# Chunks and halves of the second and third batch, and a new DVE order in the last batch, in an attention and two-level MoE kernel

## The chip, the cores and the metric

One core of a Trainium2 chip runs the program. The metric is the device time of one execution in microseconds (us): the median of three runs of the kernel before is 514.22, from 513.57 to 514.29.

## The reference, cut to what matters

Eight batches of 576 tokens go through attention with eight heads of 64, in which keys and values are means over 8 neighbours (72 of each). The 4608 rows of 512 numbers that come out go through a mixture of experts: a group is chosen, then one of its four experts, and the output is scaled by both probabilities.

```python
scores = scale * np.matmul(q, k_p.transpose(0, 1, 3, 2))
scores = scores - np.max(scores, axis=-1, keepdims=True)
attn = np.exp(scores); attn = attn / (np.sum(attn, axis=-1, keepdims=True) + 1e-09)
out_attn = np.matmul(attn, v_p)
...
h = np.maximum(xg[mask_e] @ w1[g, e], 0.0)
ye = h @ w2[g, e]
out[tok_idx] = combined[:, None] * ye
```

## The kernel before, in words

A batch goes through two stages that overlap with its neighbours: the attention of batch b+1 runs between the expert products of batch b. One main expert is taken for a whole batch (its number steers the loads of the weights); the few tokens that belong to another are gathered at the end, in a part that the code calls `Left`.

**Order.** Every engine executes its instructions in the order in which they were written. That order stands in strings of pieces: START and FIRST (batch 0), SECOND (batch 1), STEADY (batches 2 to 6), LAST (batch 7). `run` (L953) reads a string and calls one method per piece. The letter ahead of the dot says whose: `a` attention of the batch, `n` of the next, `x` of the one after that, `m` the batch's expert products, `w` those of the next, `p` of the one before, `l` the `Left` part. `n.sc:2` is thus the score products of chunk 2 of the next batch.

**Attention.** Tokens come in chunks: a batch below EARLY (3) has five, of 128 (the last 64); the others have three, of 192. For a chunk, DVE transposes q (`qb`, L322), TensorE makes the scores (`sc`, L336: per 32 tokens eight products of 72 columns), DVE takes the maxima (`mx`, L348) and subtracts them (`sd`, L357), ACT does exp (`ex`, L362), DVE sums and inverts (`su_`, L368 to L370), POOL normalises (`nm`, L375), DVE transposes the probabilities (`pt`, L382). The piece `sb` is `sd` and `ex` in one. Then TensorE multiplies with the values for half a batch at a time (`av`, L396): halves of 256 and 320 tokens in the batches below EARLY, of 288 and 288 in the others. ACT and DVE make a high and a low part of the result (L401, `avd` L412 or L414).

**Experts.** `load` brings a quarter of a weight matrix by SP, `cast` (ACT, L579) takes its high part and `lo` (L585, on POOL, or on DVE with `:v`) the remainder. `up:f:h` is 12 products for slice f of the hidden layer and half h of the tokens (L602), then relu on ACT (L604). `upd:f:h` is DVE's low part of the result (one instruction at L610 for half 0, three at L615 for half 1). Three PSUM banks are shared by the groups of 12 products, so the fourth group behind needs a bank that ACT and DVE have read out. `down` (L631, L642) is the second matrix.

**The last batch.** While TensorE does batch 7's experts, `Left` is planned, all of it on DVE but for small things: the generator `place` (L708 to L772) gives one step per `l.step` (copies of products at L734, running sums at L738 and L739, positions at L751 to L760). `which` (L774) computes on DVE which batch and which expert come next; SP reads these numbers into registers (L786 to L788), and then `fetch_x` (L834) issues two DMAs that are addressed by them. `xtiles` clears their targets by two POOL memsets (L824). When they have landed, `whole` (L848, POOL for odd chunks, DVE for even) adds the two parts and `turn` (L858) transposes them on TensorE. These transposes stand in TensorE's order between `up:7:1`, the products of `rows` (L816), and `down:12`.

Of the kernel before, what the change touches and what calls it, by code (L numbers as in the profile page):

```python
# [1000 lines left out]
```

## Time and profile before

| | |
|---|---|
| median of three runs | 514.22 us (513.57 to 514.29) |
| profiled execution | 514.15 us |
| its span | 512.4 us |
| mean granted clock of TensorE | 0.993 |
| busy: PE / PEld | 501.1 us (98%) / 440.1 us (86%) |
| busy: DVE / ACT / POOL | 345.6 (67%) / 206.3 (40%) / 281.6 us (55%) |

PE is TensorE's products, PEld its weight loads, which overlap the products; DVE, ACT and POOL are the other three engines, SP issues DMAs. The span runs from the first to the last instruction; the execution's time is 1.75 us longer. Since products are pipelined, their recorded durations overlap, and a group's cost is read from the distance between two starts. In the rows of the timeline a bracket gives the idle time ahead of the group and what ended it.

### The profile page before, as it was taken

To read this page: it belongs to the slowest core of one execution; us is meant where nothing else is said; L and a number is where in the kernel's file an instruction comes from. 1 tells how busy PE (TensorE), PEld (TensorE's weight loads), DVE (VectorE), ACT (ScalarE), POOL (GpSimd) and SP (SyncE) were. 2 spreads that over 40 slices of the span, in tenths; PEclk is the share of its full clock that TensorE was granted. 3 is DMA by queue.
4 is the path that set the end of the run, shared out by engine and by line. 5 is a ranking of instruction groups with operands and counts; after the bars stand their busy time and mean duration, and the time that the engine had idled before them with its cause. 6 is when DMAs were issued, how large, how long until landed. Compare 5 with 4: busy or idle time off the path is not lost.

```text
span 512.4 us, 14902 instructions
## 1 busy us (share of the span) xinstructions
PE 501.1 (98%) x6085; PEld 440.1 (86%) x6085; DVE 345.6 (67%) x928; ACT 206.3 (40%) x385; POOL 281.6 (55%) x246
## 2 busy tenths in 40 slices
PE   8899999999999999999999999999999999998996
PEld 6688987998889978899789988899789988898976
DVE  6876877899385869486784768476784764199702
ACT  2354432545216542455216551455325551344212
POOL 2386666576518595476828585476947471830400
PEclk9799999999999999999999999999999999999999
DMA  8699299685428966954197615985055100923751
GB/s 279 191 260 205 24 280 236 124 192 137 77 92 242 265 106 176 318 150 80 29 308 213 151 26 138 368 311 89 1 191 192 43 3 22 304 96 114 271 172 58
DMA packets 118110, 83.70 MB, mean 163 GB/s; under 512 B 71034, under 2 KB 93818, under 8 KB 117784
## 3 DMA queue, kind: packets, MB, share of 16 engines
q1 hardware_dynamic: 113408, 75.67, 54.7%
q10 hardware_dynamic: 4600, 7.02, 4.0%
q8 instruction: 49, 0.80, 0.7%
q14 instruction: 21, 0.17, 0.1%
q0 software_dynamic: 32, 0.04, 0.0%
HBM read 77.28 MB, written 28.53 MB: 206 GB/s over the span
## 4 chain that ended last, share of the span: by engine, by line
PE 76%; DVE 10%; DMA 5%; ACT 2%; POOL 2%; issue 2%; SPq 1%; ACTq 0%; DVEq 0%; POOLq 0%
PE mm L602 30%; PE mm L631 27%; PE mm L642 4%; PE sc L396 4%; PE sc L336 4%; DMA vv<-in_v_dram 2%; DMA sw<-in_moe_w_dram 2%; PE tp L429 1%; PE mm L663 1%; POOL w L585 1%; DVE s L368 1%; DVE ht L615 1%; DVE pT L382 1%; PE tp L425 1%; DVE p L357 1%
## 5 line engine op out<-in xcount | busy, mean ns | idle before, releaser
L631 PE MATMUL mm<-w,ht 128*128 128x512 f32 x744 | 172.6, 385 | 0.0
L585 POOL TENSOR_TENSOR w<-sw,w 128x1024 fp32r<-128x1024 f32 (+2 forms) x86 | 145.2, 1711 | 33.7 <-ACT w L579 29.2
L631 PEld LDWEIGHTS mm<-w,ht 128*128 128x128 f32 x744 | 136.8, 189 | 25.2 <-issue 6.4
L602 PE MATMUL mm<-xb,w 128*128 128x288 f32 (+1 forms) x768 | 109.6, 294 | 1.7 <-DVE ht L610 1.7
L602 PEld LDWEIGHTS mm<-xb,w 128*128 128x128 f32 x768 | 100.7, 189 | 6.1 <-ACT w L579 2.2
L602 PE MATMUL mm<-xa,w 128*128 128x288 f32 (+1 forms) x768 | 100.2, 283 | 0.5 <-ACT xa L401 0.5
L602 PEld LDWEIGHTS mm<-xa,w 128*128 128x128 f32 x768 | 95.5, 190 | 2.2 <-ACT xa L401 0.9
L604 ACT ACTIVATE ht<-mm 128x288 fp32r<-128x288 f32 (+2 forms) x128 | 51.9, 410 | 87.1 <-PE mm L602 85.4
L375 POOL TENSOR_TENSOR p<-p,su 128x864 f32<-128x864 f32 (+2 forms) x30 | 40.3, 1343 | 78.6 <-DVE su L370 67.7
L579 ACT CAST w<-sw 128x1024 fp32r<-128x1024 f32 x64 | 66.7, 1042 | 31.5 <-DMA sw<-in_moe_w_dram 29.0
L615 DVE SCALAR_TENSOR_TENSOR ht<-mm,ht 128x64 fp32r<-128x64 f32 (+4 forms) x192 | 37.7, 252 | 25.8 <-ACT ht L604 25.5
L636 ACT ACTIVATE y<-mm,gm 128x512 f32<-128x512 f32 x31 | 21.2, 684 | 66.4 <-PE mm L631 66.4
L362 ACT ACTIVATE p<-p 128x864 f32<-128x864 f32 (+2 forms) x30 | 23.4, 780 | 37.5 <-DVE p L357 29.6
L368 DVE TENSOR_REDUCE s<-p 128x12 f32<-128x864 f32 (+2 forms) x30 | 25.8, 861 | 15.1 <-ACT p L362 15.1
L382 DVE STREAM_TRANSPOSE pT<-p 128x960 f32<-128x960 f32 (+2 forms) x30 | 29.2, 972 | 8.0 <-POOL p L375 7.2
L610 DVE SCALAR_TENSOR_TENSOR ht<-mm,ht 128x288 fp32r<-128x288 f32 (+1 forms) x64 | 26.9, 422 | 10.4 <-ACT ht L604 10.4
L642 PE MATMUL mm<-w,ht 128*128 128x512 f32 x128 | 29.5, 381 | 0.0
L336 PEld LDWEIGHTS sc<-kT,qT 64*32 64x32 f32 x2176 | 23.7, 105 | 6.3 <-issue 3.5
L336 PE MATMUL sc<-kT,qT 64*32 64x72 f32 x2176 | 28.5, 229 | 0.5 <-DVE qT L322 0.2
L675 DVE TENSOR_TENSOR y<-mm,y 64x512 f32<-64x512 f32 x8 | 5.5, 682 | 33.6 <-ACT y L647 20.2
L396 PE MATMUL sc<-pT,v 32*64 32x288 f32 (+2 forms) x384 | 26.9, 409 | 0.2 <-DVE p L357 0.2
L396 PE MATMUL tp<-pT,v 32*64 32x288 f32 (+2 forms) x384 | 26.9, 409 | 0.0
(227 smaller groups left out, 568.8 us busy)
## 6 DMA issues: line engine op xcount, KB each, us to landing
sw<-in_moe_w_dram SPq DMA_DIRECT2D x72, 512.0 KB
vv<-in_v_dram SPq DMA_DIRECT2D x27, 320.0 KB
q<-in_q_dram SPq DMA_DIRECT2D x112, 72.0 KB
kv<-in_k_dram SPq DMA_DIRECT2D x14, 512.0 KB
out_dram<-y ACTq DMA_DIRECT2D x23, 256.0 KB
xscr<-xa SPq DMA_DIRECT2D x5, 1152.0 KB
xscr<-xb SPq DMA_DIRECT2D x5, 1152.0 KB
xscr<-xb SPq DMA_DIRECT2D x3, 1280.0 KB
```

Source lines behind the costliest of these rows:

```text
L336: nc.tensor.matmul(ps[x][32 * g:32 * g + 32, SP * t:SP * t + SP], lhsT=s.qT[c][64 * x:64 * x + 64, g, 32 * t:32 * t + 32], rhs=s.kT[64 * x ...
L368: red(out=two[:, :, :, 0], in_=p.rearrange("p t (x s) -> p t x s", x=2), axis=AX.X, op=ALU.add)
L375: (nc.vector if eng == "v" else nc.gpsimd).tensor_tensor(out=p, in0=p, in1=bc(s.su[c][:, 0:w], SP), op=ALU.mult)
L382: nc.vector.transpose(out=s.pT[:, :, o:o + n].rearrange("p j (t i) -> p t j i", i=32), in_=probs[:, z:z + n // 32].rearrange("p t (j i) -> ...
L396: nc.tensor.matmul(banks[a][64 * x:64 * x + 64, 0:n], lhsT=s.v6[32 * a:32 * a + 32, 5 if x and i == 0 else j, :], rhs=s.pT[32 * a:32 * a + ...
L579: nc.scalar.copy(out=s.w[m, j][0], in_=raw)
L585: (nc.vector if eng == "v" else nc.gpsimd).tensor_tensor(out=wl[:, i:i + n], in0=s.raw[m, j][:, i:i + n], in1=wh[:, i:i + n].bitcast(F32), ...
L602: nc.tensor.matmul(ps[:, 0:n], lhsT=l[:, kc, fs], rhs=apart(s.a.xt[hf][:, r, kc]), start=(kc == 0 and i == 0), stop=(kc == 3 and i == 2))
L604: nc.scalar.activation(out=halves(ht[:, sl]), in_=joined(ps[:, 0:n]), func=AF.Relu)
L615: stt(out=ht[:, at:at + hi - lo], in0=ps[:, a, lo:hi], scalar=0.0, in1=ht[:, t + lo:t + hi].bitcast(F32), op0=ALU.max, op1=ALU.subtract)
L631: nc.tensor.matmul(ps, lhsT=s.ht[f][:, 640 * l + o:640 * l + o + 128], rhs=apart(s.w[2, f // 2][r][:, f % 2, :]), start=(i == 0), stop=(i ...
L642: nc.tensor.matmul(ps, lhsT=s.ht[f][:, 512:640], rhs=apart(s.w[2, f // 2][r][:, f % 2, :]), start=(i == 0), stop=(i == 15))
```

## The change

EARLY becomes 1, so that batches 1 and 2 have three chunks of 192 and halves of 288. The old way of routing and of the low part stays for batches below 3, under the new name OLD. FIRST and SECOND lose the pieces of chunks 3 and 4, and others move. LAST is written anew, and so are the first two steps of `place`. One line less stands ahead of the functions, so a line of before has a number lower by one after the change.

```diff
-EARLY = 3
+EARLY, OLD = 1, 3
...
-m.lo:2:2:p:2 n.kt m.cast:2:3 m.up:5:1 m.upd:5:1 a.count a.gm_:p a.keep_x n.sc:0 n.mx:0 n.sb:0 n.qb:1 m.lo:2:3:p:2 m.up:6:1 ...
+m.lo:2:2:p:2 n.kt m.cast:2:3 m.up:5:1 m.upd:5:1 a.count a.gm_:p a.keep_x m.lo:2:3:p:2 m.up:6:1 w.load:1:0 w.load:1:1 m.upd:6:1 n.sc:0 n.mx:0 n.sb:0 n.qb:1 m.up:7:1 m.upd:7:1 n.su_:0 n.nm:0:p
...
+m.down:0 w.load:1:2 m.down:1 w.load:1:3 n.sc:1 n.pt:0 n.mx:1 n.sb:1 n.qb:2 m.down:2 m.store:0 n.su_:1 n.nm:1:p x.load_v x.load_k m.down:3 w.split:1:0:p:2 m.down:4 n.sc:2 n.mx:2 n.pt:1 n.sb:2 w.split:1:1:p:2
...
 LAST = """
-m.load:2:3 m.load:2:2 m.up:0:0 p.tail m.upd:0:0 m.lo:1:2:v m.up:0:1 l.step m.upd:0:1 m.up:1:0 l.step l.step m.upd:1:0 m.up:1:1 l.step l.step m.upd:1:1 l.xtiles
-m.up:2:0 m.cast:2:1 l.step m.upd:2:0 l.step m.up:2:1 l.step m.upd:2:1 l.step m.up:3:0 l.step l.step m.upd:3:0 m.up:3:1 l.step l.step m.upd:3:1
-m.up:5:0 l.step l.step l.step l.step m.upd:5:0 m.lo:1:3 m.cast:2:2 m.up:4:0 l.step l.step l.which m.lo:2:2:v m.upd:4:0 m.lo:2:1:v
-m.up:6:0 m.cast:2:0 m.upd:6:0 m.up:5:1 m.lo:2:0:v m.up:4:1 m.up:6:1 m.cast:2:3 l.fetch_x l.tiles m.upd:5:1 m.upd:4:1 m.upd:6:1 l.slots m.down:0 m.down:1 l.fetch_a:1
+l.step m.load:2:3 m.load:2:2 m.lo:1:2 m.lo:1:3 m.up:0:0 p.tail m.upd:0:0 m.up:0:1 l.step m.cast:2:0 m.upd:0:1 m.lo:2:0 m.up:1:0 l.step l.step m.upd:1:0 m.up:1:1 l.step l.step m.upd:1:1 l.xtiles
+m.up:2:0 m.cast:2:1 l.step m.upd:2:0 m.lo:2:1:v m.up:2:1 l.step m.upd:2:1 m.up:3:0 l.step l.step m.upd:3:0 m.up:3:1 l.step l.step m.cast:2:2 m.upd:3:1
+m.up:5:0 l.step l.step m.upd:5:0 m.up:4:0 l.step l.step l.step l.step m.upd:4:0 m.up:6:0 l.step m.upd:6:0 m.up:5:1 l.step l.which m.upd:5:1 m.up:4:1 m.lo:2:2:v m.upd:4:1 m.up:6:1 m.cast:2:3 l.fetch_x l.tiles m.upd:6:1 l.slots m.down:0 m.down:1 l.fetch_a:1
...
-                if s.b < EARLY:
+                if s.b < OLD:
...
             nc.gpsimd.affine_select(out=tri, in_=ones, ...)
+            nc.gpsimd.iota(s.colf, [[0, 4], [1, BS]], ...)
+            yield
             nc.scalar.copy(out=trir, in_=tri)
             nc.scalar.copy(out=onesr, in_=ones)
             yield
-
-            nc.gpsimd.iota(s.colf, [[0, 4], [1, BS]], ...)
```

POOL at the end of batch 6 and the start of batch 7, before; the rows are engine-order rows of line, operation, output, inputs and tile, and an `x3` is three alike in a row. `w` is the remainder of a weight quarter, `pT` and `xr` the targets of `fetch_x`:

```order
L585 TENSOR_TENSOR w<-sw,w 128x1024 x2
L715 AFFINE_SELECT kb<-ones 128x128
L720 IOTA kb 128x128
L824 MEMSET pT 128x2304
L824 MEMSET xr 128x2304
L585 TENSOR_TENSOR w<-sw,w 128x1024
L764 IOTA meta 128x8
```

The same place after the change:

```order
L584 TENSOR_TENSOR w<-sw,w 128x1024 x2
L714 AFFINE_SELECT kb<-ones 128x128
L715 IOTA kb 128x128
L584 TENSOR_TENSOR w<-sw,w 128x1024 x3
L823 MEMSET pT 128x2304
L823 MEMSET xr 128x2304
L763 IOTA meta 128x8
```

The three remainders of quarters 1:2, 1:3 and 2:0 now stand ahead of the two memsets; before, one (1:3) stood behind them.

DVE in batch 7 before, from `upd:2:1` on, with `which` (L778 to L785) and the remainders (L585):

```order
L615 SCALAR_TENSOR_TENSOR ht<-mm,ht 128x64
L738 TENSOR_TENSOR kv<-kv 128x8x16
L739 TENSOR_TENSOR kv<-kv 128x8x16
L745 TENSOR_SCALAR vv<-kv 128x128
...
L785 TENSOR_SCALAR ki<-ki 128x1
L585 TENSOR_TENSOR w<-sw,w 128x1024
L610 SCALAR_TENSOR_TENSOR ht<-mm,ht 128x288
L585 TENSOR_TENSOR w<-sw,w 128x1024
L610 SCALAR_TENSOR_TENSOR ht<-mm,ht 128x288
L585 TENSOR_TENSOR w<-sw,w 128x1024
```

DVE in batch 7 after the change, from the first pair of running sums on:

```order
L737 TENSOR_TENSOR kv<-kv 128x8x16
L738 TENSOR_TENSOR kv<-kv 128x8x16
L609 SCALAR_TENSOR_TENSOR ht<-mm,ht 128x288
L584 TENSOR_TENSOR w<-sw,w 128x1024
L737 TENSOR_TENSOR kv<-kv 128x8x16
L738 TENSOR_TENSOR kv<-kv 128x8x16
L614 SCALAR_TENSOR_TENSOR ht<-mm,ht 128x144
...
L759 TENSOR_SCALAR pos<-pos 128x40
L609 SCALAR_TENSOR_TENSOR ht<-mm,ht 128x288
L767 MEMSET it 128x1
```

A remainder (that of quarter 2:1) now stands between `upd:2:0` and the other three pairs of running sums; of the three remainders that stood right behind `which`, one is left there, and `upd:4:0` and `upd:6:0` (L609) now stand ahead of `which`.

DVE in batch 0 during `down`, after the change; `mx`, `p`, `su`, `pT` and `qT` are pieces of the next batch's attention:

```order
L367 TENSOR_REDUCE s<-p 128x12
L368 TENSOR_REDUCE su<-s 128x12
L369 RECIPROCAL su<-su 128x12
L381 STREAM_TRANSPOSE pT<-p 128x6x5x32
L347 TENSOR_REDUCE mx<-sc 128x12
L356 TENSOR_TENSOR p<-sc,mx 128x2x6x72
L321 STREAM_TRANSPOSE qT<-q 128x4x192
```

The transpose of chunk 0's probabilities (L381) now stands ahead of chunk 1's maxima; before, it stood behind the maxima and the subtraction (L348, L357).

## Rows read from the trace of the kernel before

**Rows 1.** Page, part 1: busy us, share of the span, instructions.

```profile
PE 501.1 (98%) x6085; PEld 440.1 (86%) x6085; DVE 345.6 (67%) x928; ACT 206.3 (40%) x385; POOL 281.6 (55%) x246
```

**Rows 2.** Timeline of PE, batches 1 to 3: start, us, what, count, idle before.

```profile
106.83 0.89 PE L336 MATMUL sc<-kT,qT 64*32 64x72 f32 x64
107.65 1.60 PE L602 MATMUL mm<-xa,w 128*128 128x256 f32 x12
...
121.69 0.45 PE L396 MATMUL sc<-pT,v 32*64 32x256 f32 x4 [0.16 <-DVE p L357]
...
125.25 0.48 PE L336 MATMUL sc<-kT,qT 64*32 64x72 f32 x32 [0.18 <-DVE xa L412]
...
165.67 1.50 PE L602 MATMUL mm<-xa,w 128*128 128x256 f32 x12
167.00 1.80 PE L602 MATMUL mm<-xb,w 128*128 128x320 f32 x12
168.64 1.50 PE L602 MATMUL mm<-xa,w 128*128 128x256 f32 x12
170.35 1.21 PE L336 MATMUL sc<-kT,qT 64*32 64x72 f32 x96 [0.21 <-DVE qT L322]
...
276.77 1.21 PE L336 MATMUL sc<-kT,qT 64*32 64x72 f32 x96
277.91 1.74 PE L602 MATMUL mm<-xb,w 128*128 128x288 f32 x12
```

**Rows 3.** Timeline of DVE, batch 0's second matrix.

```profile
71.74 0.85 DVE L382 STREAM_TRANSPOSE pT<-p 128x640 f32<-128x640 f32 x1 [1.33 <-POOL p L375]
```

**Rows 4.** Timeline of PE in the last batch.

```profile
455.71 1.63 PE L602 MATMUL mm<-xb,w 128*128 128x288 f32 x12
457.18 1.63 PE L602 MATMUL mm<-xa,w 128*128 128x288 f32 x12
...
467.84 3.24 PE L602 MATMUL mm<-xb,w 128*128 128x288 f32 x24 [1.68 <-DVE ht L610]
...
477.53 1.26 PE L816 MATMUL tp<-kT,q 128*128 128x2 f32 x10
478.79 1.09 PE L858 MATMUL tp<-ident,pT 128*128 128x128 f32 x8
```

**Rows 5.** Timeline of DVE in the last batch.

```profile
450.34 2.69 DVE L585 TENSOR_TENSOR w<-sw,w 128x1024 fp32r<-128x1024 f32 x1
...
457.82 0.59 DVE L615 SCALAR_TENSOR_TENSOR ht<-mm,ht 128x144 fp32r<-128x144 f32 x3
458.32 0.28 DVE L738 TENSOR_TENSOR kv<-kv 128x128 f32<-128x128 f32 x1
...
466.20 1.22 DVE L585 TENSOR_TENSOR w<-sw,w 128x1024 fp32r<-128x1024 f32 x1
467.33 0.45 DVE L610 SCALAR_TENSOR_TENSOR ht<-mm,ht 128x288 fp32r<-128x288 f32 x1
```

**Rows 6.** Timeline of POOL, last batch and start of the program.

```profile
2.57 1.18 POOL L117 MEMSET p<- 128x1280 f32 x1
...
446.65 2.01 POOL L824 MEMSET xr<- 128x2304 f32 x1
449.58 2.36 POOL L585 TENSOR_TENSOR w<-sw,w 128x1024 fp32r<-128x1024 f32 x1 [0.92 <-ACT w L579]
...
477.23 3.18 POOL L848 TENSOR_TENSOR pT<-pT,xr 128x512 f32<-128x512 f32 x2 [23.83 <-DMA xr<-xscr]
```

**Rows 7.** Timeline of DVE, start of the program.

```profile
2.77 1.01 DVE L104 SCALAR_TENSOR_TENSOR inside<-at,inside 128x10 f32<-128x10 f32 x1
```

**Rows 8.** Timeline of ACT in the last batch.

```profile
451.60 0.30 ACT L717 CAST v<-ones 128x128 fp32r<-128x128 f32 x1
456.21 1.04 ACT L579 CAST w<-sw 128x1024 fp32r<-128x1024 f32 x1
```

**Rows 9.** Windows: bounds, length, busy of PE, PEld, DVE, ACT, POOL, PEclk, DMA share, GB/s.

```profile
20.00:25.00 5.00, 4.38 (x75) 3.66 (x76) 4.12 (x9) 3.22 (x6) 3.79 (x6) 0.54 1.01 325
```

More of the change, by code (lines that the diff above doesn't have):

```diff
@@ L46 @@
 m.up:0:1:1 m.upd:0:1 n.kr:1 a.rt:1 n.guess_x m.cast:2:0 m.up:1:1 n.guess_e m.upd:1:1 a.route_g m.cast:2:1 m.up:2:1 m.upd:2:1 a.route_e:p a.gates m.lo:2:0:p:2 m.up:3:1 m.upd:3:1 m.lo:2:1:p:2 m.cast:2:2 m.up:4:1 n.qb:0 m.upd:4:1
-m.lo:2:2:p:2 n.kt m.cast:2:3 m.up:5:1 m.upd:5:1 a.count a.gm_:p a.keep_x n.sc:0 n.mx:0 n.sb:0 n.qb:1 m.lo:2:3:p:2 m.up:6:1 w.load:1:0 w.load:1:1 m.upd:6:1 n.su_:0 n.nm:0:p m.up:7:1 m.upd:7:1
-m.down:0 w.load:1:2 n.sc:1 n.mx:1 n.sb:1 n.pt:0 n.qb:2 m.down:1 w.load:1:3 m.down:2 m.store:0 n.su_:1 n.nm:1:p x.load_v x.load_k w.split:1:0:p:2 m.down:3 n.sc:2 n.pt:1 n.mx:2 n.sb:2 n.qb:3 n.qb:4 m.down:4 n.su_:2 n.nm:2:p w.split:1:1:p:2
@@ new lines @@
+m.down:0 w.load:1:2 m.down:1 w.load:1:3 n.sc:1 n.pt:0 n.mx:1 n.sb:1 n.qb:2 m.down:2 m.store:0 n.su_:1 n.nm:1:p x.load_v x.load_k m.down:3 w.split:1:0:p:2 m.down:4 n.sc:2 n.mx:2 n.pt:1 n.sb:2 w.split:1:1:p:2
+m.down:5 m.store:1 m.down:6 n.av:0 n.su_:2 n.nm:2:p n.avd:0 m.down:7 x.load_qb:0 m.down:8 m.store:2 x.vr:0 n.rt:0 w.load:2:0 w.load:2:1 n.pt:2 m.down:9 x.kr:0 n.av:1 n.avd:1 m.down:10 x.kr:1 x.vr:1 x.vm x.load_qb:1 x.load_qb:2 x.load_qb:3 n.rt:1 m.down:11 m.store:3 n.route_g n.route_e:p m.down:12 n.gates n.gm_:p m.down:13 m.store:4
@@ L50 @@
 """
 SECOND = """
-m.up:0:0 m.upd:0:0 n.qb:0 m.up:1:0 m.upd:1:0 m.split:1:2:p:2 m.load:2:2 a.count n.kt m.up:0:1 m.upd:0:1 a.keep_x m.split:1:3:p:2 m.load:2:3 m.up:1:1 m.upd:1:1 n.sc:0 n.mx:0 n.sb:0 n.qb:1 m.up:2:0 m.upd:2:0 n.su_:0 n.nm:0:p m.split:2:0:p:2 m.up:2:1 m.upd:2:1 n.sc:1 n.mx:1 n.sb:1 n.pt:0 n.qb:2
-x.load_v m.up:3:0 m.upd:3:0 n.su_:1 n.nm:1:p m.split:2:1:p:2 m.up:3:1 m.upd:3:1 m.up:4:0 m.upd:4:0 n.sc:2 n.mx:2 n.sb:2 n.pt:1 n.qb:3 x.load_k m.split:2:2:p:2 m.up:4:1 m.upd:4:1 n.su_:2 n.nm:2:p m.up:5:0 m.upd:5:0 m.up:5:1 m.upd:5:1 n.sc:3 n.mx:3 n.sb:3 n.pt:2 n.qb:4
@@ L54 @@
-x.load_qb:0 x.load_qb:1 x.load_qb:2 x.load_qb:3 m.up:6:0 m.upd:6:0 n.su_:3 n.nm:3:p m.up:7:0 m.upd:7:0 n.av:0 n.avd:0 m.split:2:3:p:2 m.up:6:1 m.upd:6:1 n.sc:4 n.mx:4 n.sb:4 n.pt:3 m.up:7:1 m.upd:7:1 n.su_:4 n.nm:4:p m.down:0 n.pt:4 x.vr:0 m.down:1 x.vr:1 x.vm m.down:2 m.store:0 m.down:3 n.av:1 n.avd:1
-m.down:4 x.kr:0 n.rt:0 n.rt:1 m.down:5 m.store:1 n.route_g n.route_e:p x.kr:1 m.down:6 m.down:7 x.qb:0 m.down:8 m.store:2 x.kt n.main_expert w.load:1:0 w.load:1:1 w.load:1:2 w.load:1:3 n.gates n.gm_ n.keep_x m.down:9 w.split:1:0:p:2 w.load:2:0
+m.up:0:0 m.upd:0:0 n.qb:0 m.up:1:0 m.upd:1:0 m.split:1:2:p:2 m.load:2:2 a.count n.kt m.up:0:1 m.upd:0:1 a.keep_x m.split:1:3:p:2 m.load:2:3 m.up:1:1 m.upd:1:1 n.sc:0 n.mx:0 m.up:2:0 m.upd:2:0 n.sd:0 n.ex:0 n.qb:1 m.up:2:1 m.upd:2:1 n.su_:0 n.nm:0:p m.split:2:0:p:2
@@ new lines @@
+x.load_v m.up:3:0 m.upd:3:0 m.up:3:1 m.upd:3:1 n.sc:1 n.pt:0 n.mx:1 m.up:4:0 m.upd:4:0 n.sd:1 n.ex:1 n.qb:2 x.load_k m.up:4:1 m.upd:4:1 n.su_:1 n.nm:1:p m.split:2:1:p:2 m.up:5:0 m.upd:5:0 m.split:2:2:p:2 m.up:5:1 m.upd:5:1 n.sc:2 n.pt:1 n.mx:2
+x.load_qb:0 x.load_qb:1 x.load_qb:2 x.load_qb:3 m.up:6:0 m.upd:6:0 n.sd:2 n.ex:2 m.up:7:0 m.upd:7:0 m.up:6:1 m.upd:6:1 n.su_:2 n.nm:2:p m.split:2:3:p:2 m.up:7:1 m.upd:7:1 n.av:0 n.avd:0 m.down:0 n.pt:2 x.vr:0 m.down:1 x.vr:1 x.vm n.av:1 n.avd:1 m.down:2 m.store:0 x.kr:0 n.rt:0
@@ L56 @@
+m.down:3 n.rt:1 m.down:4 n.route_g n.route_e:p x.kr:1 m.down:5 m.store:1 m.down:6 x.qb:0 m.down:7 x.kt n.main_expert w.load:1:0 w.load:1:1 w.load:1:2 w.load:1:3 n.gates n.gm_ n.keep_x m.down:8 m.store:2 m.down:9 w.split:1:0:p:2 w.load:2:0
 x.sc:0 x.mx:0 x.sb:0 m.down:10 x.qb:1 m.down:11 m.store:3 w.split:1:1:p:2 w.load:2:1 x.su_:0 x.nm:0:p m.down:12 w.cast:1:2 m.down:13 m.store:4
@@ L422, in rt @@
             ps = ps_t.tile([128, 512], F32, name="tp")
-            if s.b < EARLY:
+            if s.b < OLD:
                 for i in range(8):
@@ L451, in route_g @@
             lg = lgs[b % 2]
-            if b < EARLY:
+            if b < OLD:
                 lp = ps_t.tile([128, 512], F32, name="tp")
@@ L715, in place @@
             nc.gpsimd.affine_select(out=tri, in_=ones, pattern=[[1, 128]], compare_op=ALU.is_gt, fill=0.0, base=0, channel_multiplier=-1)
+            nc.gpsimd.iota(s.colf, [[0, 4], [1, BS]], base=0, channel_multiplier=0, allow_small_or_imprecise_dtypes=True)
+            yield
             nc.scalar.copy(out=trir, in_=tri)
@@ L718, in place @@
             yield
-            nc.gpsimd.iota(s.colf, [[0, 4], [1, BS]], base=0, channel_multiplier=0, allow_small_or_imprecise_dtypes=True)
             sl = sq.tile([128, NC * DM], F32, name="q")
@@ L953, in run @@
     def run(plan, b):
-        who = dict(a=att[b], m=moe[b], n=att[b + 1], w=moe[b + 1], p=moe[b - 1] if b else None, x=att[b + 2], y=att[b + 2] if b == EARLY - 1 else None, r=moe[b] if b == EARLY - 1 else None, z=att[b + 3], t=top, l=left)
+        who = dict(a=att[b], m=moe[b], n=att[b + 1], w=moe[b + 1], p=moe[b - 1] if b else None, x=att[b + 2], y=att[b + 2] if b == OLD - 1 else None, r=moe[b] if b == OLD - 1 else None, z=att[b + 3], t=top, l=left)
         for piece in plan.split():
```

1 line of the change is left out of this document (removed).

## The prediction

> **What bounds the kernel now.** I read the page's busy times first: PE is busy 98% of the span [rows 1], so the time is what TensorE has to do plus the few places where it stands. DVE, ACT and POOL count only where TensorE, or a transfer that TensorE needs, ends up waiting for them. So I went through the timeline of PE for two things: what a group costs (distance of starts), and brackets.
>
> In batches 1 and 2 three brackets are seen: 0.16 us at the values, 0.18 and 0.21 us at the scores, all ended by DVE [rows 2]. In the last batch one is large: 1.68 us at 467.84, ended by the low part of a hidden slice on DVE [rows 4]. It looks like the thing to remove. But one row further on in the program says what it is worth: POOL's first addition starts at 477.23, released by the landing of `fetch_x` after 23.83 us of idleness [rows 6], and the transposes that need it start on PE at 478.79, just where the products of `rows` end (477.53 + 1.26) [rows 4]. TensorE and the landing arrive there within about 0.2 us of each other. If TensorE came 2 us earlier it would wait 2 us for the landing. The landing hangs on `which`: DVE finishes it at 466.20, where the next remainder starts [rows 5], then SP reads registers and issues, and the data come. From the end of `which` to the transposes are 478.79 − 466.20 = 12.6 us, of which nothing is touched by the change. So **the last batch ends by DVE's `which`**, not by the 1.68 us.
>
> **The change part by part.**
>
> *Halves.* Twelve products cost 1.33 us for 256 columns (165.67 to 167.00) and 1.64 for 320 (167.00 to 168.64) [rows 2], 2.97 the pair; for 288 columns 1.47 (455.71 to 457.18) [rows 4], 2.94 the pair. Eight pairs in each of batches 1 and 2: −0.24 each.
>
> *Chunks.* Scores of 128 tokens cost 0.82 (106.83 to 107.65), of 192 tokens 1.14 (276.77 to 277.91) [rows 2]. Four of 0.82 and a half one are 3.69, three of 1.14 are 3.42: −0.27 per batch whose attention changes, that is once in FIRST (batch 1's) and once in SECOND (batch 2's). Each visit also costs at its entry: from 168.64 to 170.35 are 1.71, less the twelve products (1.33) and the bracket (0.21) leaves 0.17 [rows 2]. Two visits fewer: about −0.3 in each of FIRST and SECOND. It could be nothing.
>
> *Brackets in batches 1 and 2.* The scores and values are visited later against DVE's work, so I let 0.16 + 0.18 go in batch 1 and 0.21 in batch 2.
>
> *New waits in batch 0.* In FIRST, DVE's transpose of chunk 0's probabilities now stands ahead of chunk 1's maxima. It waits for POOL's normalisation; a wait of that kind was 1.33 us [rows 3]. Behind it are queued the maxima, the subtraction and the transpose of q that the next scores need, so TensorE can come to wait. From below it is nothing, since two groups of `down` lie between; from above 1.33 at each of two places, or 2.7. I take 0.5, near the lower end, as the products in between are longer than the wait.
>
> Sum of the early batches: FIRST −0.27 − 0.3 + 0.5 = −0.1; SECOND −0.24 − 0.27 − 0.3 − 0.34 = −1.15; batch 2 −0.24 − 0.21 = −0.45. Together **−1.7**, between −2.4 (no new waits, 0.2 of other small ones gone) and −0.5 (no gain at visits, more waits).
>
> *Last batch, POOL.* Of the remainders, 1:2 and 2:0 go from DVE to POOL, and the two memsets now stand behind three remainders. Quarter 2:0's cast follows ACT's copies, which end at 451.90 [rows 8]; with 1.04 for a cast [rows 8] it ends at 452.94. POOL is free by then (its remainder of 1:3 ended at 451.94 [rows 6], and stays about there). A remainder on POOL is 2.36, so 2:0 ends at 455.3, and the memsets, 2.01 each [rows 6], run to 457.3 and 459.2. Before, they were over at 448.66, and DVE's long run had not begun.
>
> *Last batch, DVE.* The remainder of 2:1 is now ahead of three of the running-sum pairs and so ahead of `which`. It needs its cast, which ends at 457.25 [rows 8]. Alone it takes 1.13 (466.20 to 467.33). But beside POOL's remainder the same instruction took 2.69: from 450.34 to 453.03, 1.09 after POOL's ended at 451.94 [rows 5, 6]. It was held for as long as POOL ran. A memset holds too: at the start, an addition of 10 columns took 1.01 us and ended at 3.78, when a memset that began at 2.57 ended at 3.75 [rows 6, 7]. So here the remainder of 2:1, ready at 457.25, falls into the second memset and ends about 1.1 after it, at 460.3. Behind it stand the same instructions that ran from 457.82 to 466.20 before [rows 5], 8.38; plus two pairs of running sums that ran ahead of 457.82 before, at most 4 × 0.28 [rows 5]; plus `upd:4:0` and `upd:6:0`, 0.45 each by their record [rows 5], 0.37 when the overlap of records is taken off as the remainder's shows it (1.22 against 1.13). That is 8.4 + 1.0 + 0.75 = 10.15, so `which` ends at 470.45 against 466.20: **+4.25**. DVE has no slack to take it up: it works without a bracket over that stretch, and the two remainders that are now behind `which` never stood ahead of it.
>
> The Trainium skill, "GPSIMD Engine Reference", § 8 Key points, says that POOL shares its SBUF interfaces with VectorE and that contention falls on VectorE's instructions with two SBUF inputs (or in a 2-port mode). It does not say what POOL must be doing; read narrowly, a memset, which reads nothing, would leave the remainder alone, and the sum would be the unheld one below, 514.8. The row at the start speaks against that reading.
>
> *Last batch, the rest.* `fetch_x`, its landing, POOL's and DVE's additions and PE's transposes follow `which` at the same distance: from 478.79 to 483.0. TensorE has them ahead of `down:12` in its order and no slack behind, so the end moves by +4.25. The 1.68 us at 467.84 shrinks or goes; it is worth nothing, as TensorE then waits at 478 for the landing.
>
> **Sum**: −1.7 + 4.25 = +2.55, on the profiled execution's 514.15: **516.7**. That execution lies 0.07 below the median, which I neglect. A measurement of this kernel can tell about 0.2%, 1.03 us.
>
> **The rivals.**
>
> *The remainder is not held.* The memset's hold rests on one row at the start, with small instructions; and if the remainder gets in ahead of the second memset, POOL waits instead. DVE's lead decides: 457.25 against the second memset's start at 457.3 or a little less is close, but a pair of running sums that the first memset holds would delay the remainder past it. Without the hold it ends at 458.4, `which` at 468.55, +2.35: 514.15 − 1.7 + 2.35 = 514.8, within 0.2%. Chance 0.2.
>
> *TensorE's clock falls in the new gap.* With the landing at 483 TensorE stands some 4 us ahead of the transposes, behind ten products of 2 columns [rows 4]. In this trace the granted clock was 0.54 from 20 to 25 us [rows 9], the lower of the two levels (1.2 GHz), after a stretch of small products with gaps. A similar spell behind the gap costs half of up to 5 us, 2.5: 519.2. Against it: the 1.68 us left the clock alone (the mean is 0.993). Chance 0.2. The Trainium skill, "TensorE: Matmul & The Clock Gate", § Why this matters for your kernels, advises to leave no idle gap between bursts of products, or the clock falls to its lower level. By that rule the time would be this rival's.
>
> *Faster: the landing does not bind.* This wants that the transposes wait for TensorE's own arrival alone and that `which` is not later, say because ACT makes the cast of 2:1 earlier or DVE catches up while TensorE is slow. Then the last batch gives back its 1.68 us and some 0.3 behind it: 514.15 − 1.7 − 2.0 = 510.4. It decides at a landing before about 476.6, so `which` before 464.0; even without any hold I count 468.5. Chance 0.12, for an error in that count.
>
> *New waits in batches 0 and 1.* If both places of FIRST cost their 1.33 and the visits give nothing, the early batches come to +1 instead of −1.7, and the time to 519.4. Chance 0.05.
>
> **How the numbers follow.** The forecast has 0.43: 516.7, by its bounds from 515.6 to 518.0. With 0.2 at 514.8, 0.2 at up to 519.2, 0.12 at 510.4 and 0.05 at 519.4, a range from 513.8 to 519.2 leaves out the faster case and a little at the top. Faster by over 0.2% (under 513.1): 0.13. Within 0.2% (to 515.2): the unheld case and a little of the forecast, 0.22. Slower: 0.65.
>
> **What would show it.** Right: the start of batch 3's first slice about 1.7 us earlier; in the last batch the memsets on POOL between 455 and 459; one DVE remainder of some 3 us ending about 460; `which` near 470 less the 1.7; a bracket of 4 us on PE ahead of the transposes, with POOL's addition released by the landing. Wrong: a remainder of 1.2 us there (no hold), or `which` earlier than 464 and transposes without a bracket ahead (the faster rival); a PEclk under 0.9 near the end (the clock).

## The result, and the profile after

The changed kernel is slower: 519.33 us median of 5 runs (517.57 to 520.63) against 514.22, a ratio of 1.0095 (95% interval 1.0075 to 1.0115). The profiled execution took 517.91 us, its span is 516.2 against 512.4. Stage by stage, from the starts of the first slice of each batch in the timeline of PE (over the profiles of this case the first slice of batch 0 starts at 25.5 to 27.8 us, so stages are compared by their lengths):

| stage, us | before | after | forecast of the difference | measured |
|---|---|---|---|---|
| batch 0, from its first slice | 68.67 | 69.52 | −0.1 | +0.85 |
| batch 1 | 62.30 | 62.91 | −1.15 | +0.61 |
| batch 2 | 58.67 | 58.15 | −0.45 | −0.52 |
| batches 3 to 6 | 230.71 | 230.72 | 0 | 0 |
| last batch, to the end of the span | 64.63 | 68.32 | +4.25 | +3.69 |

The stages add up to +4.63 us. The spans differ by 3.8, since batch 0 started 0.84 us earlier after the change (26.58 instead of 27.42), and the profiled execution lies 1.4 us below the median of the changed kernel.

PE in batches 0 to 2 after the change (start, us, what, idle before and what ended it):

```profile
72.09 1.20 PE L335 MATMUL sc<-kT,qT 64*32 64x72 f32 x96 [0.61 <-DVE qT L321]
...
77.87 0.47 PE L395 MATMUL sc<-pT,v 32*64 32x288 f32 x4 [0.93 <-DVE p L356]
...
121.84 0.77 PE L601 MATMUL mm<-xa,w 128*128 128x288 f32 x5 [0.76 <-issue]
...
131.72 0.47 PE L395 MATMUL sc<-pT,v 32*64 32x288 f32 x4 [0.75 <-DVE pT L381]
```

The three brackets of before [rows 2] are gone, and four larger ones have come, two in each of batches 0 and 1. What DVE did ahead of the first two, from its timeline:

```profile
67.84 1.18 DVE L381 STREAM_TRANSPOSE pT<-p 128x960 f32<-128x960 f32 x1 [1.81 <-POOL p L374]
68.95 1.02 DVE L347 TENSOR_REDUCE mx<-sc 128x12 f32<-128x864 f32 x1
70.00 1.06 DVE L356 TENSOR_TENSOR p<-sc,mx 128x864 f32<-128x864 f32 x1
70.98 0.97 DVE L321 STREAM_TRANSPOSE qT<-q 128x768 f32<-128x768 f32 x1
...
75.45 1.18 DVE L381 STREAM_TRANSPOSE pT<-p 128x960 f32<-128x960 f32 x1 [0.90 <-POOL p L374]
76.66 1.06 DVE L356 TENSOR_TENSOR p<-sc,mx 128x864 f32<-128x864 f32 x1
```

DVE stood 1.81 and 0.90 us ahead of the transposes of probabilities, waiting for POOL's normalisation, with the transpose of q (for the next scores) and the subtraction (which frees the PSUM that the values need) queued behind. These answer to [rows 3].

The last batch after the change, PE, then DVE, then POOL:

```profile
475.64 1.26 PE L815 MATMUL tp<-kT,q 128*128 128x2 f32 x10
480.98 1.96 PE L857 MATMUL tp<-ident,pT 128*128 128x128 f32 x8 [4.07 <-POOL pT L847]
482.59 2.88 PE L641 MATMUL mm<-w,ht 128*128 128x512 f32 x8
```

```profile
457.39 1.23 DVE L584 TENSOR_TENSOR w<-sw,w 128x1024 fp32r<-128x1024 f32 x1 [0.48 <-ACT w L578]
...
464.31 0.45 DVE L609 SCALAR_TENSOR_TENSOR ht<-mm,ht 128x288 fp32r<-128x288 f32 x1
...
466.48 0.45 DVE L609 SCALAR_TENSOR_TENSOR ht<-mm,ht 128x288 fp32r<-128x288 f32 x1
...
468.45 0.57 DVE L614 SCALAR_TENSOR_TENSOR ht<-mm,ht 128x144 fp32r<-128x144 f32 x3
```

```profile
457.29 2.02 POOL L823 MEMSET xr<- 128x2304 f32 x1
...
479.42 3.17 POOL L847 TENSOR_TENSOR pT<-pT,xr 128x512 f32<-128x512 f32 x2 [18.65 <-DMA xr<-xscr]
```

The 1.68 us of [rows 4] is gone, and a bracket of 4.07 us stands ahead of the transposes, released by POOL's addition, which was released by the landing at 479.4 instead of 477.2 [rows 6]. `which` ends at 468.45, where L614 starts, instead of 466.20 [rows 5], with two low parts (464.31, 466.48) now ahead of it; 0.11 of this is the later start of the batch. DVE's remainder took 1.23 us in the midst of the second memset: **it was not held**. And behind the gap the eight products of L641 take 2.88 us instead of some 1.97. The windows view shows why (bounds, length, busy of PE, PEld, DVE, ACT, POOL with counts, PEclk, DMA share, GB/s):

```profile
478.00:480.00 2.00, 0.00 (x0) 0.00 (x0) 0.62 (x2) 0.00 (x0) 0.58 (x1) 1.00 0.99 360
480.00:482.00 2.00, 1.02 (x5) 0.99 (x6) 1.97 (x7) 0.00 (x0) 2.00 (x2) 0.75 1.09 349
482.00:484.00 2.00, 2.00 (x8) 1.64 (x7) 1.86 (x5) 0.58 (x1) 2.00 (x2) 0.50 0.48 156
484.00:486.00 2.00, 2.00 (x13) 1.74 (x12) 1.97 (x7) 0.00 (x0) 0.91 (x1) 0.89 0.06 9
```

After four idle microseconds the granted clock is 0.50, the lower of its two levels, and comes back in the window up to 486. From the transposes to the end of the span are 35.22 us (516.2 − 480.98) instead of 33.61 (512.4 − 478.79): the clock cost 1.6 us here. (Against 33.81 us, the same distance in the run below in which `which` stands early and the clock stays at 1.00, it is 1.4.) The five runs had mean clocks of 0.996, 0.996, 0.992, 0.990 and 0.989 and took 517.91, 517.57, 520.63, 519.33 and 519.58 us; that the three longer ones lost more to the clock at the same place is likely, but not shown, as only the first has a trace.

### The profile page after: what moved, and what is told of

Its sections match the earlier page's. It is cut to its first block, busy times and chain, and to the rows that moved or that the text cites. A ratio compares the mean times of both kernels' runs of the same rounds, so it can differ in the third digit from the quotient of the medians.

```text
span 516.2 us, 14853 instructions
## 1 busy us (share of the span) xinstructions
PE 500.0 (97%) x6085; PEld 440.3 (85%) x6085; DVE 340.6 (66%) x898; ACT 205.9 (40%) x381; POOL 285.9 (55%) x244
## 4 chain that ended last, share of the span: by engine, by line
PE 81%; DVE 9%; ACT 3%; DMA 2%; POOL 2%; issue 1%; SPq 1%; POOLq 0%; ACTq 0%
PE mm L601 29%; PE mm L630 28%; PE mm L641 6%; PE sc L395 4%; PE sc L335 4%; PE mm L946 2%; DMA xr<-xscr 1%; DVE p L356 1%; POOL p L374 1%; PE tp L428 1%; DVE ht L614 1%; PE tp L424 1%; DVE pT L381 1%; PE mm L662 1%; DVE s L367 1%
## 5 line engine op out<-in xcount | busy, mean ns | idle before, releaser
L584 POOL TENSOR_TENSOR w<-sw,w 128x1024 fp32r<-128x1024 f32 (+2 forms) x88 | 149.7, 1725 | 43.3 <-ACT w L578 43.3
L630 PEld LDWEIGHTS mm<-w,ht 128*128 128x128 f32 x744 | 136.8, 189 | 25.4 <-issue 6.7
L601 PE MATMUL mm<-xb,w 128*128 128x288 f32 (+1 forms) x768 | 106.6, 291 | 0.0
L601 PE MATMUL mm<-xa,w 128*128 128x288 f32 (+1 forms) x768 | 102.6, 286 | 1.6 <-ACT xa L400 0.9
L601 PEld LDWEIGHTS mm<-xb,w 128*128 128x128 f32 x768 | 98.6, 189 | 3.7 <-ACT w L578 2.2
L601 PEld LDWEIGHTS mm<-xa,w 128*128 128x128 f32 x768 | 97.2, 189 | 3.4 <-ACT xa L400 1.3
L578 ACT CAST w<-sw 128x1024 fp32r<-128x1024 f32 x64 | 66.5, 1041 | 32.8 <-DMA sw<-in_moe_w_dram 30.4
L614 DVE SCALAR_TENSOR_TENSOR ht<-mm,ht 128x64 fp32r<-128x64 f32 (+4 forms) x192 | 37.2, 249 | 25.7 <-ACT ht L603 25.7
L635 ACT ACTIVATE y<-mm,gm 128x512 f32<-128x512 f32 x31 | 21.2, 685 | 62.7 <-PE mm L630 62.7
L609 DVE SCALAR_TENSOR_TENSOR ht<-mm,ht 128x288 fp32r<-128x288 f32 (+1 forms) x64 | 27.5, 431 | 13.2 <-ACT ht L603 13.2
L381 DVE STREAM_TRANSPOSE pT<-p 128x960 f32<-128x960 f32 (+2 forms) x26 | 28.6, 1099 | 9.6 <-POOL p L374 9.0
L641 PE MATMUL mm<-w,ht 128*128 128x512 f32 x128 | 30.3, 389 | 0.0
L641 PEld LDWEIGHTS mm<-w,ht 128*128 128x128 f32 x128 | 24.6, 195 | 3.8 <-issue 0.2
L347 DVE TENSOR_REDUCE mx<-sc 128x12 f32<-128x864 f32 (+2 forms) x24 | 23.7, 988 | 5.2 <-PE sc L335 5.2
```

The lines of the kernel that those rows point to most:

```text
L381: nc.vector.transpose(out=s.pT[:, :, o:o + n].rearrange("p j (t i) -> p t j i", i=32), in_=probs[:, z:z + n // 32].rearrange("p t (j i) -> ...
L578: nc.scalar.copy(out=s.w[m, j][0], in_=raw)
L584: (nc.vector if eng == "v" else nc.gpsimd).tensor_tensor(out=wl[:, i:i + n], in0=s.raw[m, j][:, i:i + n], in1=wh[:, i:i + n].bitcast(F32), ...
L601: nc.tensor.matmul(ps[:, 0:n], lhsT=l[:, kc, fs], rhs=apart(s.a.xt[hf][:, r, kc]), start=(kc == 0 and i == 0), stop=(kc == 3 and i == 2))
L614: stt(out=ht[:, at:at + hi - lo], in0=ps[:, a, lo:hi], scalar=0.0, in1=ht[:, t + lo:t + hi].bitcast(F32), op0=ALU.max, op1=ALU.subtract)
L630: nc.tensor.matmul(ps, lhsT=s.ht[f][:, 640 * l + o:640 * l + o + 128], rhs=apart(s.w[2, f // 2][r][:, f % 2, :]), start=(i == 0), stop=(i ...
```

## The experiments

Theory A: the loss is made in the last batch, by a chain from `which` over the landing to a gap on TensorE and its clock. Theory B: the new waits of batches 0 and 1 carry it.

**The change without its last batch, and its last batch alone.** In the first, LAST (all five lines) and the first two steps of `place` are as before; in the second, the same lines the other way, only these are new.

```diff
 LAST = """
-l.step m.load:2:3 m.load:2:2 m.lo:1:2 m.lo:1:3 m.up:0:0 p.tail m.upd:0:0 m.up:0:1 l.step m.cast:2:0 ...
+m.load:2:3 m.load:2:2 m.up:0:0 p.tail m.upd:0:0 m.lo:1:2:v m.up:0:1 l.step m.upd:0:1 ...
...
```

> The changed kernel with the LAST plan and the first steps of place as before; batches 0 to 2 as changed. Theory A (the loss is made in the last batch: which ends 2.25 us later, the landing follows, TensorE stands 4 us and its clock falls behind that): 514.3 us, the kernel before plus the 0.1 by which the last batch started later in the changed kernel's profile; no gap over 2 us and no clock below full speed behind 470 us. Theory B (the new waits of batches 0 and 1, 0.61 + 0.93 + 0.76 + 0.75 us, carry the loss): 517 us, with the same four brackets. A middle value would split the loss.

> The kernel before with the new LAST plan and the new first steps of place alone; batches 0 to 2 as before. Theory A: as much slower as the changed kernel is, 517.5 to 520.5 us, with a bracket of 4 us ahead of the transposes and a lower clock behind it. Theory B: 514 us, or 516.4 if only the later landing (2.2 us) and no clock is lost.

Measured: without it 515.01 us, ratio 1.0015 (0.9996 to 1.0033); alone 517.62 us, 1.0068 (1.0049 to 1.0087). Stages: 69.53, 62.91, 58.38 and 64.49 us in the first, 68.68, 62.32, 58.88 and 68.29 in the second. The stages go with their plans, and four fifths of the loss by stages (3.7 of 4.6 us) is the last batch's: theory A. The early batches lose too, about 1 us by their stages (0.94 in the changed kernel, 1.18 here), where they were to gain 1.7; by the times alone, with an interval from 0.9996, that loss would not be shown. PE of the first run, then of the second, at the transposes:

```profile
479.06 1.26 PE L816 MATMUL tp<-kT,q 128*128 128x2 f32 x10
480.25 1.09 PE L858 MATMUL tp<-ident,pT 128*128 128x128 f32 x8
```

```profile
474.26 1.26 PE L815 MATMUL tp<-kT,q 128*128 128x2 f32 x10
479.72 1.97 PE L857 MATMUL tp<-ident,pT 128*128 128x128 f32 x8 [4.19 <-POOL pT L847]
```

**Work put into the gap.** Two pieces of the second matrix go ahead of the transposes.

```diff
-m.up:7:0 l.fetch_b:1 m.upd:7:0 l.whole:4 ... m.upd:7:1 l.turn:3 l.turn:4 m.down:12
-... l.whole:2 m.lo:2:3:p m.down:2 m.down:3 l.turn:2 m.down:4 ... m.down:8 l.down ... m.down:13 m.down:9
+m.up:7:0 l.fetch_b:1 m.upd:7:0 m.lo:2:3:v l.whole:4 ... m.upd:7:1 m.down:12 m.down:2 l.turn:3 l.turn:4 m.down:3
+... l.whole:2 m.down:4 l.turn:2 m.down:5 ... m.down:13 l.down ... m.down:9
```

> The changed kernel, with two pieces of the second matrix (3.5 us) moved ahead of the transposes on TensorE, and the remainder of 2:3 on DVE ahead of the additions so that they can run there. Which, the landing and the transposes' earliest time stay. Theory A: the gap shrinks from 4.07 to about 0.5 us and the clock does not fall: 517.9 - 3.5 - 1.7 = 512.7 us, faster than both kernels. Rival (TensorE waits for the chain of the leftover part anyway, so that a gap only moves to a later step): 516 to 518 us, with a new bracket behind 481 us.

Measured: 516.83 us, 1.0057 (1.0031 to 1.0082), the rival's time, though its new bracket on TensorE did not come. The gap is 1.94 us and the clock stays at 1.00 behind it, as theory A has it, but the gain is lost at the end. The chain that ended last (start, us, what):

```profile
473.32 9.09 DMA xr<-xscr
...
498.68 1.93 PE mm L630 x8
...
504.67 3.18 DMA out_dram<-y
...
508.96 2.64 DMA out_dram<-q,idx
```

Two things are to be seen. The transfer of `xr` took 9.09 us from its issue, 1.5 more than in the changed kernel (7.57, from its issue at 471.72). And `down:13`, which I had put ahead of the leftover part's last step, stores rows of the output; the leftover's own scatter into the output waited for that store (504.67 + 3.18, then 508.96), and ACT's last piece of the output waited 4.23 us for the scatter. So the last store is issued at 512.56 us, as in the changed kernel (512.53), though TensorE ends 2 us earlier. My edit had made a new wait. The run shows a gap of 2 us without a fall of the clock, and that the leftover's chain is close behind TensorE at the end.

**One remainder behind `which`.**

```diff
-m.up:2:0 m.cast:2:1 l.step m.upd:2:0 m.lo:2:1:v m.up:2:1 ... l.which m.upd:5:1 m.up:4:1
+m.up:2:0 m.cast:2:1 l.step m.upd:2:0 m.up:2:1 ... l.which m.upd:5:1 m.lo:2:1:v m.up:4:1
```

> The changed kernel with DVE's remainder of 2:1 (1.13 us) behind which instead of ahead of it. If which sets the landing one to one: which ends about 467.3 instead of 468.45 in the changed kernel's time, the gap ahead of the transposes is 2.9 instead of 4.07 us, and the time falls by 1.1 us, to 516.8 against the changed profile's 517.9; if a gap of 2.9 us leaves the clock alone, by 1.7 to 4 us more (515 or less). If the landing hangs on something else, no change.

Measured: 519.24 us, 1.0114 (1.0070 to 1.0159); a miss. From the batch's first slice (448.68) `which` ends after 20.1 instead of 20.6 us: DVE then waits for ACT's relu where it had the remainder to do, so the end moves by 0.5, not 1.1. TensorE comes to the transposes earlier too (28.8 instead of 29.0 us behind that slice, and the transposes start at 32.8 instead of 33.1), and the gap stays at 4.01 us. It was no separation of the theories.

**`which` where its inputs are ready.** It needs the running sum over experts alone. Its registers' counter and loop count move there as well.

```diff
             nc.vector.tensor_tensor_scan(out=s.cum, ...)
+            nc.vector.memset(s.it, 0.0)
+            ts(out=s.tmp[:, 0:1], in0=s.cum[:, B * NE - 1:B * NE], ...)
+            nc.vector.tensor_copy(out=s.niti, in_=s.tmp[:, 0:1])
+            yield
             tt(out=exc..., in0=s.cum, in1=nb, op=ALU.subtract)
-            yield
...
-m.up:5:0 l.step l.step m.upd:5:0 ... m.up:5:1 l.step l.which m.upd:5:1
+m.up:5:0 l.step l.which l.step m.upd:5:0 ... m.up:5:1 l.step m.upd:5:1
```

> The changed kernel; which stands right behind the running sum over experts, the last thing it needs, instead of behind all the positions. Theory A (which sets the landing and the landing the gap): which ends about 4 us earlier (from the last batch's first slice 16.6 instead of 20.6 us), the transposes start 29.5 us behind it instead of 33.1, with under 0.5 us of gap, the clock stays, and the last batch takes 62.7 us instead of 68.3 (64.6 before the change): 512.7 us, faster than both kernels. Rival (the landing hangs on something else, such as SP's queue or the memsets): the gap stays at 3 to 4 us.

Measured: 513.60 us, 0.9979 (0.9956 to 1.0003): the whole loss of the change is back. That is 0.9 us more than expected, as the last batch is 1 us longer than the 62.7 us expected. From the batch's first slice (449.04) `which` ends after 16.3 us (465.36), the last batch takes 63.66 us, and the clock is 1.00 throughout. DVE's first instruction behind `which`, POOL's first addition and PE:

```profile
465.36 0.28 DVE L755 TENSOR_TENSOR vv<-cum,vv 128x128 f32<-128x128 f32 x1
```

```profile
476.38 2.68 POOL L846 TENSOR_TENSOR pT<-pT,xr 128x512 f32<-128x512 f32 x2 [14.42 <-DMA xr<-xscr]
```

```profile
466.39 5.08 PE L601 MATMUL mm<-xb,w 128*128 128x288 f32 x36 [0.42 <-DVE ht L609]
...
477.70 1.26 PE L814 MATMUL tp<-kT,q 128*128 128x2 f32 x10
478.89 1.09 PE L856 MATMUL tp<-ident,pT 128*128 128x128 f32 x8
```

The landing is 2.5 us ahead of the transposes and TensorE has no bracket there; a small one of 0.42 us where the low part of slice 5 now waits behind `which`. This settles theory A: only `which` and what it computes with were moved.

**The same move in the kernel before.**

```diff
-m.up:3:1 l.step l.step m.upd:3:1 ... m.up:4:0 l.step l.step l.which m.lo:2:2:v
+m.up:3:1 l.step l.which l.step m.upd:3:1 ... m.up:4:0 l.step l.step m.lo:2:2:v
```

> The kernel before with nothing changed but which, right behind the running sum over experts. Theory A (in the kernel before, the landing and TensorE, with its 1.68 us, arrive at the transposes together, so that taking away one of the two gives nothing): which ends about 4 us earlier, the landing comes 4 us before it is needed, the 1.68 us stays near 468 us, and the time is the same within 0.5 us of 514.2. Rival (the landing alone sets the end): 512 us or less.

Measured: 515.09 us, 1.0019 (1.0003 to 1.0035): no gain, as theory A has it, but a loss of 1 us, twice what I allowed. Of it 0.4 is in the last batch (65.00 instead of 64.63 us); the rest lies in stages that the edit does not touch (batch 2 took 59.35 us, with a bracket of 0.90 us where the kernel before has the 0.21 of [rows 2]). PE and DVE:

```profile
468.66 3.24 PE L602 MATMUL mm<-xb,w 128*128 128x288 f32 x24 [1.21 <-DVE ht L610]
...
479.21 0.92 PE L815 MATMUL tp<-kT,q 128*128 128x2 f32 x6 [0.35 <-DVE q L809]
```

```profile
474.52 5.02 DVE L809 TENSOR_SCALAR q<-kb,kT 128x128 f32<-128x128 f32 x5
```

TensorE's wait for DVE stays (0.22 + 1.21 instead of 1.68 us). So in the kernel before, the landing and TensorE's own lateness are two bounds of nearly the same height. The five instructions of L809 took 5.02 instead of 1.06 us: the earlier landing put POOL's additions (474.26 to 476.76) and its next remainder (to 479.07) beside them.

**The waits of batch 0.**

```diff
-n.sc:1 n.pt:0 n.mx:1 n.sb:1 n.qb:2 m.down:2 ... m.down:6 n.av:0 n.su_:2 n.nm:2:p n.avd:0 m.down:7
+n.sc:1 n.mx:1 n.qb:2 n.pt:0 n.sb:1 m.down:2 ... m.down:6 n.su_:2 n.nm:2:p m.down:7 n.av:0 n.avd:0
```

> The changed kernel; in FIRST the maxima of chunk 1 and the transpose of q stand ahead of the transpose of chunk 0's probabilities on DVE, and the values of the first half one piece of the second matrix later. If the two new brackets of batch 0 (0.61 and 0.93 us in the changed kernel) come from that transpose waiting for POOL's normalisation: both go, batch 0's first slice to batch 1's takes 68.0 instead of 69.5 us, and the time falls by 1.5 us. Rival (the wait moves to the values' second half, whose probabilities come later): 69 us or more.

Measured: batch 0 takes 68.05 us, both brackets gone, as expected to 0.05 us. The time is 517.25 us, 1.0057 (1.0038 to 1.0076), against 1.0095 for the change. In this profile the gap ahead of the transposes is 4.36 us, and the lower clock lasts longer than in the changed kernel's; from the transposes to the end are 35.98 us instead of 35.22 (columns as in the windows above):

```profile
476.00:480.00 4.00, 0.00 (x0) 0.00 (x0) 1.58 (x2) 0.00 (x0) 1.53 (x2) 0.75 1.03 375
480.00:484.00 4.00, 3.98 (x14) 3.35 (x15) 3.80 (x11) 0.58 (x1) 3.95 (x2) 0.50 0.48 152
```

**The waits of batch 1.**

```diff
-n.sc:2 n.pt:1 n.mx:2 ... m.upd:6:0 n.sd:2 n.ex:2 ... m.down:1 x.vr:1 x.vm n.av:1 n.avd:1 m.down:2 m.store:0
+n.sc:2 n.mx:2 ... m.upd:6:0 n.pt:1 n.sd:2 n.ex:2 ... m.down:1 m.down:2 m.store:0 x.vr:1 x.vm n.av:1 n.avd:1
```

> The changed kernel; in SECOND the transpose of chunk 1's probabilities stands behind the maxima of chunk 2 and the low part of slice 6 on DVE instead of ahead of them, and the values of the second half one piece of the second matrix later. If the brackets of batch 1 come from DVE waiting there for POOL: the 0.76 us (idle with no releaser shown) and the 0.75 us go, batch 1's first slice to batch 2's takes 61.4 instead of 62.9 us, and the time falls by 1.5 us. Rival (the 0.76 us is a late fetch of instructions, which DVE's order does not touch): only 0.75 us are gained, 62.15 us.

Measured: 62.21 us, the rival's 62.15; 517.69 us, 1.0072 (1.0052 to 1.0091). DVE's order took away the 0.75, not the idle time without a releaser:

```profile
120.87 0.77 PE L601 MATMUL mm<-xa,w 128*128 128x288 f32 x5 [0.48 <-issue]
...
131.50 0.70 PE L630 MATMUL mm<-w,ht 128*128 128x512 f32 x2 [0.32 <-POOL w L584]
```

**All three edits** (batch 0, batch 1, `which`).

> The changed kernel with all three edits (batch 0's waits, batch 1's waits, which early). Theory A: the gains add up: 68.0 + 61.4 + 58.15 us for batches 0 to 2 (189.6 before the change, 187.6 here) and 62.7 us for the last (64.6): some 4 us below the kernel before, 510.2 us. If they share a slack: 511 to 513 us.

Measured: 511.29 us, 0.9954 (0.9938 to 0.9969); stages 68.05, 62.20, 58.15, and 63.45 for the last. The gains that the three edits had alone add up (68.05, 62.21 and 63.66 us there). The time lies in the range expected for a shared slack, because batch 1 and the last batch each stay 0.8 us above the length expected for them.

**The idle time without a releaser.** In the changed kernel SP issues q's 16 loads for batch 3 from 117.1 us, in the kernel before from 122.6; a fetch of instructions (16 KB on queue 8) is on the DMA engines between 119 and 120 us, and between 118 and 119 before. The edit, on top of all three, holds the loads back:

```diff
-x.load_qb:0 x.load_qb:1 x.load_qb:2 x.load_qb:3 m.up:6:0 ... m.down:2 m.store:0 x.vr:1
+m.up:6:0 ... m.down:2 m.store:0 x.load_qb:0 x.load_qb:1 x.load_qb:2 x.load_qb:3 x.vr:1
```

> The kernel with all three edits; SP's 16 loads of q for batch 3 stand behind the first store of batch 1, so that they are issued from about 131 us instead of 117 us. If the idle 0.70 us without a releaser in batch 1 (0.48 to 1.09 us in the other runs) is a fetch of instructions that lands late behind the loads' small packets: no gap there, batch 1 takes 61.5 instead of 62.20 us, and the time falls by 0.7 us to 510.6 us. Rival (the gap is of the code at that place, whatever the loads do): still a gap of 0.5 to 1.1 us near 121 us. A miss of another kind would be a new wait near 145 us, for q landing late.

Measured: the gap near 121 is gone, but batch 1 still takes 62.19 us, and the time is 511.22 us, 0.9936 (0.9915 to 0.9957). A wait that had been hidden came out:

```profile
129.72 0.92 PE L630 MATMUL mm<-w,ht 128*128 128x512 f32 x3 [0.34 <-POOL w L584]
130.96 0.70 PE L630 MATMUL mm<-w,ht 128*128 128x512 f32 x2 [0.32 <-POOL w L584]
```

That the gap hangs on the loads is likely, but not shown. Of the nine profiles with the loads in their early place, seven have it, with 0.21 to 1.09 us, and two do not (work put into the gap, the waits of batch 0); of the five with the loads later, none has it, but three of those have the order of the kernel before. That the loads' packets delay the fetch itself is only argued: the trace shows when the fetch was moved, not when it was asked for.

What the runs do show is that the gap cost nothing. In the six profiles with the changed kernel's order of batch 1 it is 0, 0, 0.21, 0.48, 0.76 and 1.09 us, and the batch takes 62.90 to 62.92 us in all six; in the four with DVE's new order and POOL's old one it is 0 to 0.70 us, and the batch takes 62.19 to 62.21. What holds the changed kernel there is DVE: its transpose waits for POOL, with the maxima and the low part of slice 6 queued behind, and TensorE meets that low part late even where it has no gap. First DVE in the changed kernel, then PE in the run on batch 0's waits, which has no gap:

```profile
121.40 1.18 DVE L381 STREAM_TRANSPOSE pT<-p 128x960 f32<-128x960 f32 x1 [0.75 <-POOL p L374]
122.50 1.02 DVE L347 TENSOR_REDUCE mx<-sc 128x12 f32<-128x864 f32 x1
123.44 0.44 DVE L609 SCALAR_TENSOR_TENSOR ht<-mm,ht 128x288 fp32r<-128x288 f32 x1
```

```profile
122.72 1.74 PE L601 MATMUL mm<-xb,w 128*128 128x288 f32 x12 [0.61 <-DVE ht L609]
...
130.50 0.47 PE L395 MATMUL sc<-pT,v 32*64 32x288 f32 x4 [0.76 <-DVE pT L381]
```

**The remainder of 2:1 behind `which`**, on top of all three.

```diff
-m.upd:2:0 m.lo:2:1:v m.up:2:1 ... l.step m.upd:5:1 m.up:4:1 m.lo:2:2:v
+m.upd:2:0 m.up:2:1 ... l.step m.lo:2:1:v m.upd:5:1 m.up:4:1 m.lo:2:2:v
```

> The kernel with all three edits; DVE's remainder of 2:1 behind which and the positions instead of ahead of them. If it is what delays the low part that TensorE waits for in the last batch (0.43 and 0.13 us at 464 and 467): both go, the last batch takes 62.9 instead of 63.45 us, and the time falls by 0.5 us. Rival (DVE then waits for ACT instead, as in the run with that remainder moved alone): the two brackets stay within 0.2 us and the time is the same.

Measured: both brackets gone, the last batch takes 62.92 us, 510.85 us, 0.9930 (0.9909 to 0.9951). What was useless alone pays once `which` no longer stands behind it.

**The best version**: all three, both of the last two, and in batch 1

```diff
-n.su_:2 n.nm:2:p m.split:2:3:p:2 m.up:7:1
+n.su_:2 m.split:2:3:p:2 n.nm:2:p m.up:7:1
```

> The kernel with all three edits, with q's loads behind the first store, the remainder of 2:1 behind which, and in batch 1 POOL's remainder of 2:3 ahead of the normalisation of chunk 2 (with q's loads moved alone, the second matrix waited 0.34 + 0.32 us for that remainder). If these were the last waits of batch 1: 61.5 instead of 62.2 us, the last batch 62.9 us, and 510.1 us in all. Rival (the normalisation, later by 2.5 us, holds the transpose and the values of the second half): a new bracket of up to 1 us ahead of the values near 131 us, 510.9 us.

Measured: **510.03 us, 0.9921 (0.9896 to 0.9947)**, faster than both kernels; batch 1 takes 61.62 us, the last 62.93. Which of its two edits in batch 1 gave the 0.6 us was not separated: the loads moved alone gave nothing, and POOL's order alone was not run. One bracket of the rival's kind is left in batch 1:

```profile
130.73 0.47 PE L395 MATMUL sc<-pT,v 32*64 32x288 f32 x4 [0.50 <-DVE pT L381]
```

## Why the prediction was right or wrong

The forecast was slower, 516.7 us between 513.8 and 519.2; 1.0095 times 514.22 is 519.1, just inside the range; the median, 519.33, is just outside. The direction and the chain came out as written. Three sizes did not, and they erred against each other: the hold put 2.0 us too much into the sum, the clock's 1.6 us was left out of it, and the early batches were 2.6 us too short. That the last batch's +3.69 lies near the forecast +4.25 is luck: it is 2.1 of a later landing and 1.6 of the clock, where the forecast had the landing alone.

- *"The last batch ends by DVE's which, not by the 1.68 us": right.* With the 1.68 us gone the last batch was longer, not shorter; `which` later by 2.1 us (measured from the batch's first slice) gave a landing later by 2.1 us, and `which` earlier by 4.3 us gave the loss back. From the end of `which` to the transposes are 12.5 us (480.98 − 468.45) against 12.6 before.
- *"The memset holds the remainder", +4.25: wrong.* The remainder took 1.23 us beside a memset, here and in seven more profiles, and 2.69 beside POOL's remainder in three. The step that failed is the reading of the row at the start of the program [rows 7]: that addition stood behind a `tensor_scalar` (2.68, L113, 1.11 us) in DVE's queue, so its 1.01 us can be its neighbour's:

```profile
2.68 1.11 DVE L113 TENSOR_SCALAR hm<-flath 128x40 f32<-128x40 f32 x1
```

  The same sum without the hold gave `which` at +2.35; measured is 468.45 − 466.20 = +2.25. The narrow reading of the Trainium skill ("GPSIMD Engine Reference", § 8 Key points), by which a memset leaves a remainder alone, is the one that the row at 457.39 agrees with.
- *The clock: a rival with 0.2, and it happened* in each profile in which TensorE stood 4 us (the change, its last batch alone, and the runs with one edit of batch 0, batch 1 or the remainder), and in none where it stood 2 us or less there. I had it as a rival on top of the held case; it came with the unheld one. I priced it at 2.5; by the distance from the transposes to the end (33.61 us before) the changed profile shows 1.6, the last batch alone 1.5, and the runs on batch 0, on batch 1 and on the remainder 2.4, 1.6 and 2.2. The Trainium skill's rule ("TensorE: Matmul & The Clock Gate", § Why this matters for your kernels), to leave no idle gap between bursts of products, held, and deserved more than 0.2, since my own sum had the gap in it.
- *The early batches, −1.7: wrong, +0.9.* Halves and chunks came as priced: batch 2 gained 0.52 (0.45 forecast); with its two waits taken away batch 0 is 0.62 us shorter than before the change (0.57 priced); and batch 1 in the best version is 0.68 shorter, with a wait of 0.50 left (1.15 priced). The term that failed is "New waits in batch 0", 0.5 us: the two places cost 0.61 + 0.93. And for batch 1 there was no such term: I let the brackets of before go and looked for nothing in their place, though the same order stands there (transpose ahead of maxima): DVE waits for POOL there and TensorE for DVE, 0.75 us at the values; with DVE's order changed the batch was 0.70 us shorter. The 0.76 us without a releaser is no part of the loss, as the runs with other gaps show. I had not asked why the transposes were moved forward. In three chunks they share the probabilities' buffer: chunk 0 has slots 0 to 5 and chunk 1 slots 2 to 7, so chunk 0 has to be transposed before chunk 1 is subtracted, and q's transpose has one buffer instead of two. The larger chunks pay with slack.
